# Two parts of a decoded weight summed on TensorE, fewer and longer VectorE instructions, and a new order of the work

## The chip, the cores and the metric

The kernel runs on one core of one Trainium2 chip. The metric is the device time of one execution in microseconds, and the time before is the median of 11 runs. A core has five engines, each with its own queue of instructions: TensorE (matrix products, written PE in the profile), VectorE (DVE), ScalarE (ACT), GpSimd (POOL) and SyncE (SP), which issues most of the DMAs. An engine works off its queue in order; between engines, semaphores hold an instruction back until its inputs are written and its output buffer is free.

## The reference

```python
def _attn_ref(q, k, v, a_re, a_im):            # each (4, 8, 768, 48)
    mag = np.sqrt(a_re * a_re + a_im * a_im)
    scale = np.minimum(mag, 0.999) / (mag + 1e-06)
    a_re_n, a_im_n = (a_re * scale, a_im * scale)
    for t in range(S):
        ar, ai = (a_re_n[:, :, t, :, None], a_im_n[:, :, t, :, None])
        new_re = ar * S_re - ai * S_im
        new_im = ar * S_im + ai * S_re
        S_re, S_im = (new_re + outer(k[t], v[t]), new_im)
        y[:, :, t] = q[t] @ S_re
    ...
def _moe_ref(x, w_in, w_out):                  # x (3072, 384), (384, 2048), (2048, 384)
    h = np.maximum(x @ w_in, 0.0)
    return (h * h @ w_out).astype(np.float32)
```

A gated recurrence with complex gates runs over 768 steps for each of 4 sequences and 8 heads. Its outputs, with the heads side by side, are 3072 tokens of 384 features, which go through two layers with a squared ReLU between them. The two weight matrices come in float64; everything else is float32.

## The kernel before

The 3072 tokens are cut into 24 chunks of 128 steps; two chunks of different sequences make one of 12 groups. A chunk's recurrence is turned into products: with the running products of the gates, queries are multiplied and keys divided by them (operands), a masked score matrix is made from both, and a state per head is carried from chunk to chunk. Groups 0 to 5 run through one pair of sequences and groups 6 to 11 through the other.

All work is cut into steps, and a string FRONT (L1035) writes down in which order they are issued: `follow` (L1129) reads token after token and calls the function behind its letter. On VectorE, TensorE, SyncE and ScalarE this is the order in which each engine runs its instructions. A token is a letter, a group or block, and a step:

- `l` loads a group's gates, queries and keys into the single tile `raw` (group 0 in two parts, l0.0 the gates and l0.1 the rest; 12 to 16 DMAs), `v` its values, `f` a block of 64-bit weights into one of three `words` tiles; blocks 0 to 7 are columns of the first matrix, 8 to 15 rows of the second.
- `D` decodes a block on VectorE (`decode`, L566): two instructions make `head`, two make `rest`, a fifth adds them into the float32 weight. `W` (`watch`) scans the words on ScalarE for values out of range.
- `o` are a group's operands (`make_operands`, L656), in the list's order: 0 squares, 1 and 2 the parts put in blocks, 3 sum of squares, 4 and 5 inverse and its square, 6 queries, 7 Newton step, 8 limit, 9 lessened, 10 grown factor (all ScalarE, but for 3 and 7), 11 gates, 12 negated (ScalarE), 13 grow (a running product over each of six segments, and the keys times it), 14 keys (ScalarE), 15 and 16 the running complex products in blocks of 8, 17 totals over the blocks, 18 carries (ScalarE), 19 carried, 20 products, 21 the DMAs for the last heads. Where no engine is named it is VectorE.
- `a` and `b` are the group's first and second chunk (`chunk`, L816): 0 scores, 1 and 3 keys transposed, 6 sums over values, 8 what is added to the state (TensorE); 2, 4 and 7 copies out of PSUM (ScalarE); 5 masked scores and 9 the new state (VectorE). `g` fills the gap rows of the tokens by DMA, after which `F` may start.
- `F` is one eighth of the first layer's product (12 recorded instructions, because a float32 product is recorded as two), `H` its squared ReLU on ScalarE, `T` an eighth of the second layer for groups 0 and 1, `E` its copy, `s` the store.
- From group 2 on, `X`, `Y` and `Q` (sums of tokens on VectorE), `t` (sums of weights) and `Z` (seven half-sized products in the place of eight) make the second layer, and `R` puts its outputs together.

In PSUM the pool `pa` (L455) holds the scores of a chunk, in two tiles of one bank, and the two outputs of T1; `py` the sums over values and the outputs of T0; `pm` the transposed keys and what is added to the state. A step that writes one of these waits until the step that reads the former content is done. `F0.f` needs block f of the weights, `T0.f` and `T1.f` block 8 + f.

The complex product is written out in `cmul` (L642): two products over both parts, then a difference and a sum.

Of the kernel before, what the change touches and what calls it, by code (L numbers as in the profile page):

```python
# [23 lines left out]
I32 = mybir.dt.int32  # L24
# [401 lines left out]
def quotient_path(ctx, tc, feat, vtok, w_in, w_out, w1, w2, out, n_seq, good):  # L426
# [28 lines left out]
    pa = ctx.enter_context(tc.tile_pool(name="pa", bufs=2, space=PSUM))  # L455
# [81 lines left out]
    carry = const.tile([P, 2, SEG, NB], F32, name="carry")  # L537
    nc.vector.memset(carry[:, RE], 1.0)
    nc.vector.memset(carry[:, IM], 0.0)
# [4 lines left out]
    prod = [const.tile([P, 2, GC, NP], F32, name=f"prod{i}") for i in range(2)]  # L544
# [12 lines left out]
    ends = const.tile([P, NGR, SEG], F32, name="ends")  # L557
    sizes = const.tile([P, 2, 2 * NBLK], F32, name="sizes")
# [7 lines left out]
    def decode(dst, words, j):  # L566
# [4 lines left out]
        both = scr.tile([P, 2, E], I32, tag="work", name="decoded")  # L571
        head, rest = both[:, 0], both[:, 1]
# [9 lines left out]
        tt(dst, head.bitcast(F32), rest, ALU.add)  # L582
# [8 lines left out]
    words_of = {}  # L591
# [50 lines left out]
    def cmul(out, x, w, shape, room=None):  # L642

        p_, w_ = room or [tmp.tile([P, 2] + shape, F32, name=name) for name in ("p_", "w_")]
        tt(p_, x, w[RE], ALU.mult)
        tt(w_, x, w[IM], ALU.mult)
        tt(out[:, RE], p_[:, RE], w_[:, IM], ALU.subtract)
        tt(out[:, IM], p_[:, IM], w_[:, RE], ALU.add)

    def spread(w, shape):  # L650

        return [w[:, c].unsqueeze(1).unsqueeze(3).to_broadcast([P, 2] + shape) for c in (RE, IM)]
# [3 lines left out]
    def make_operands(gi):  # L656
# [13 lines left out]
        def steps_in_blocks(js):  # L670

            for j in js:
                ab = tiles["ab"]
                x, w = ab[:, now, j - 1], ab[:, 0:2, j]
                plane = L * n

                x = bass.AP(tensor=x.tensor, offset=x.offset + plane,
                            ap=[x.ap[0], [-plane, 2], [0, 2], [1, n]])
                w = bass.AP(tensor=w.tensor, offset=w.offset,
                            ap=[w.ap[0], [plane, 2], [plane, 2], [1, n]])  # L680
                pr = tmp.tile([P, 2, 2, n], F32, name="pr")
                tt(pr, x, w, ALU.mult)
                tt(ab[:, now, j], pr[:, 0], pr[:, 1], ALU.add)

        def squares():
            tiles["sq"] = nrm.tile([P, 2, E], F32, name="sq")
# [36 lines left out]
        def limit():  # L723
            tiles["both"] = nrm.tile([P, 2, E], F32, name="both")
# [23 lines left out]

# [462 lines left out]
```

## Time and profile before

| | us |
|---|---|
| median of 11 runs | 707.85 (706.92 to 711.58) |
| profiled execution | 707.07 |
| its span | 705.3 |
| TensorE busy | 624.3 (89%) |
| VectorE busy | 531.4 (75%) |
| ScalarE busy | 368.9 (52%) |
| GpSimd busy | 12.0 (2%) |
| DMA | 47.75 MB, 68 GB/s on average |

The span runs from the first to the last instruction of the profiled execution; its device time is 1.8 us longer. The profile's strip cuts the span into 40 slices of 17.6 us and gives the busy share of each engine in tenths. The lists of instructions by time give start, duration, engine, line, operation, the tiles written and read, and in brackets the idle time before and what ended it. Nearly all VectorE products and sums have the line of the helper `tt` (L478), so they are told apart by their tiles and sizes.

### The profile page before, as it was taken

The numbers are of one execution on the slowest core, as the hardware profiler recorded it, in microseconds if no ns is written. First come the engines' busy times: TensorE is split into PE (matmuls) and PEld (weight loads), VectorE is DVE, ScalarE is ACT, GpSimd is POOL, SyncE is SP. The second block draws the span as 40 slices with busy tenths as digits, with TensorE's granted clock in tenths as the row PEclk, the third lists the DMA queues.
The fourth block names the chain that finished last, engine by engine and source line by source line (L and its number), as shares of the span: only waits on it lengthen the run. The fifth ranks groups of instructions, "written<-read, shape, count | busy, mean of one in ns | idle before, by whom it ended". The sixth has DMA issues, their size and how long they took to land.

```text
span 705.3 us, 12538 instructions
## 1 busy us (share of the span) xinstructions
PE 624.3 (89%) x4955; PEld 547.4 (78%) x4955; DVE 531.4 (75%) x1045; ACT 368.9 (52%) x636; POOL 12.0 (2%) x36
## 2 busy tenths in 40 slices
PE   0025688999879999999999999999999999999995
PEld 0024576775668998998998988988988989989995
DVE  2999999999897887987866967868868959922020
ACT  6466387476437538348357276285285284230330
POOL 3000000000000000000000000000000000000000
PEclk9999699999999999999999999999999999999999
DMA  5985572842351061421520620711612510010101
GB/s 135 171 135 106 85 158 80 163 127 85 79 87 23 8 123 30 76 71 24 118 46 1 119 46 7 124 35 25 116 25 41 101 23 5 16 35 1 29 0 29
DMA packets 46150, 47.75 MB, mean 68 GB/s; under 512 B 6017, under 2 KB 40961, under 8 KB 46081
## 3 DMA queue, kind: packets, MB, share of 16 engines
q1 hardware_dynamic: 45600, 46.46, 34.0%
q8 instruction: 41, 0.67, 0.4%
q10 hardware_dynamic: 480, 0.39, 0.2%
q14 instruction: 29, 0.23, 0.1%
HBM read 36.18 MB, written 4.72 MB: 58 GB/s over the span
## 4 chain that ended last, share of the span: by engine, by line
PE 73%; DVE 17%; DMA 4%; SPq 3%; issue 1%; ACT 0%; DVEq 0%; ACTq 0%
PE h_ps L927 28%; PE o_ps L1002 26%; PE a_ps L845 5%; PE o_ps L943 5%; DVE ab L478 3%; PE y L871 2%; PE y L837 2%; PE add L889 2%; DVE pr L478 2%; DMA raw<-in_feat_dram 2%; PE tp L852 1%; DVE qk L478 1%; DVE w L478 1%; DVE decoded L575 1%; DVE decoded L580 1%
## 5 line engine op out<-in xcount | busy, mean ns | idle before, releaser
L927 PE MATMUL h_ps<-x,w 128*128 128x256 f32 x1152 | 261.1, 384 | 8.3 <-DMA x<-x 7.4
L927 PEld LDWEIGHTS h_ps<-x,w 128*128 128x128 f32 x1152 | 218.9, 192 | 39.6 <-DMA x<-x 5.0
L1002 PE MATMUL o_ps<-w,h 128*128 128x192 f32 x640 | 110.3, 328 | 0.0
L1002 PEld LDWEIGHTS o_ps<-w,h 128*128 128x128 f32 x640 | 104.0, 190 | 2.2 <-issue 1.5
L932 ACT ACTIVATE h<-h_ps 128x512 f32<-128x512 f32 x96 | 57.6, 600 | 89.2 <-PE h_ps L927 85.6
L478 DVE TENSOR_TENSOR mix<-h 128x256 f32<-128x256 f32 x40 | 16.9, 422 | 62.9 <-ACT h L933 62.9
L933 ACT ACTIVATE h<-h 128x512 f32<-128x512 f32 x96 | 60.6, 631 | 3.0
L667 ACT ACTIVATE qk<-raw 128x768 f32<-128x768 f32 x24 | 36.8, 1534 | 36.3 <-DMA raw<-in_feat_dram 9.5
L1002 PE MATMUL o_ps<-w_sum,mix 128*128 128x192 f32 x320 | 54.9, 329 | 0.0
L852 PE MATMUL tp<-ident,qk 128*128 128x128 f32 x120 | 22.2, 297 | 35.3 <-DVE qk L478 27.2
L1002 PEld LDWEIGHTS o_ps<-w_sum,mix 128*128 128x128 f32 x320 | 51.8, 190 | 1.4 <-issue 1.4
L478 DVE TENSOR_TENSOR pr<-ab 128x384 f32<-128x384 f32 x84 | 46.7, 556 | 2.3
L852 PEld LDWEIGHTS tp<-ident,qk 128*128 128x128 f32 x120 | 14.7, 148 | 40.9 <-ACT size L588 27.7
L478 DVE TENSOR_TENSOR qk<-ab,qk 128x768 f32<-128x768 f32 x48 | 44.9, 955 | 0.8
L943 PE MATMUL o_ps<-w,h 128*128 128x384 f32 x128 | 42.4, 488 | 1.3 <-DVE w L478 0.8
L478 DVE TENSOR_TENSOR a<-a_ps,mask 128x512 f32<-128x512 f32 x48 | 30.8, 684 | 14.8 <-PE a_ps L845 14.8
L845 PE MATMUL a_ps<-qk 48*128 48x128 f32 x576 | 40.7, 290 | 0.0
L667 ACT ACTIVATE both<-z 128x768 f32<-128x768 f32 x24 | 37.1, 1563 | 5.7 <-DVE z L718 5.7
L845 PEld LDWEIGHTS a_ps<-qk 48*128 48x128 f32 x576 | 36.0, 197 | 4.4 <-issue 4.3
L943 PEld LDWEIGHTS o_ps<-w,h 128*128 128x128 f32 x128 | 24.1, 190 | 18.0 <-DVE w L478 1.5
L667 ACT ACTIVATE ab<-raw 128x768 f32<-128x768 f32 x24 | 37.7, 1570 | 0.3 <-DVE qk L478 0.3
L871 PE MATMUL y<-a,vt 128*64 128x128 f32 x384 | 29.0, 285 | 4.8 <-DVE a L478 4.6
(299 smaller groups left out, 817.4 us busy)
## 6 DMA issues: line engine op xcount, KB each, us to landing
raw<-in_feat_dram SPq DMA_DIRECT2D x44, 288.0 KB
words<-in_moe_w_out_dram SPq DMA_DIRECT2D x8, 768.0 KB
last<-qk SPq DMA_DIRECT2D x72, 64.5 KB
vt<-in_vtok_dram SPq DMA_DIRECT2D x24, 192.0 KB
out_dram<-o SPq DMA_DIRECT2D x24, 192.0 KB
raw<-in_feat_dram SPq DMA_DIRECT2D x132, 32.0 KB
words<-in_moe_w_in_dram SPq DMA_DIRECT2D x16, 192.0 KB
words<-in_moe_w_in_dram SPq DMA_DIRECT2D x32, 96.0 KB
```

The costliest lines, as they stand in the source:

```text
L478: nc.vector.tensor_tensor(out=out, in0=in0, in1=in1, op=op)
L667: nc.scalar.activation(out=out.rearrange("p c j n -> p c n j"), func=AF.Copy, in_=in_.rearrange("p c (n j) -> p c n j", j=L), **kwargs)
L837: nc.tensor.matmul(ys[p_ % 2][crossed(hh, p_), p_ // 2], lhsT=states[b][1 - c_seq % 2][rows(hh), c, p_], rhs=operand(c, p_, rows(hh)), sta ...
L845: nc.tensor.matmul(ps[hh][:, p_], lhsT=operand(2 + c, p_, rows(hh)), rhs=operand(c, p_, rows(hh)), start=(c == RE), stop=(c == IM))
L852: nc.tensor.transpose(tp[:, g], operands[gi][:, 2 + c, b, g, 0:C], ident)
L871: nc.tensor.matmul(tiles["y"][p_ % 2][crossed(hh, p_), p_ // 2], lhsT=v[:, at:at + ROWS], rhs=tiles["am"][hh][:, p_], start=(first and p_ ...
L889: nc.tensor.matmul(add[rr, c, p_], lhsT=kt[c][:, p_, rr], rhs=v[:, at:at + D], start=True, stop=True)
L927: nc.tensor.matmul(ps[:, j], lhsT=w1[:, g, (2 * f + j) * P:(2 * f + j + 1) * P], rhs=x_of[i][:, g], start=(g == 0), stop=(g == NG - 1))
L932: nc.scalar.activation(out=h, in_=h_ps[i, f], func=AF.Relu)
L933: nc.scalar.activation(out=h, in_=h, func=AF.Square)
L943: nc.tensor.matmul(o_of[i, b], lhsT=tokens_of(i, f, b)[:, j], rhs=w2[:, k], start=(k == 0), stop=(k == NFB - 1))
L1002: nc.tensor.matmul(to, lhsT=x(k)[:, j], rhs=factor(z)[:, 2 * k + j], start=(z in (0, 1, 3) and k == j == 0), stop=(k == KH // 2 - 1 and j ...
```

## The change

Seven edits:

1. `decode` writes `head` straight into the weight's place. For blocks 0 to 7 its fifth instruction is gone: step `B` (`summed`) multiplies head and rest with the unit matrix on TensorE and adds both in a PSUM tile of `pa`, and step `C` (`sums_copied`) copies that to the weight's place on ScalarE. Two blocks share one buffer for their rests.
2. `pa` has one buffer of two banks instead of two of one. Scores of both halves, the two outputs of T1 and the sums of `B` each take the whole of it. `masked` becomes one instruction over both halves.
3. `grow` scans all six segments in one instruction: step 22 on ScalarE squares the factors, copies the first one of each segment to `begun` and sets it to zero in the factors, so that the scan starts anew there.
4. `carried` and `new_state` make four products in two instructions and then one sum over both parts, with a third, negated plane in `carry` and `prod`, which ScalarE (and GpSimd for the last heads) fills.
5. `totals` makes its first level's four products in one instruction.
6. The temporary tiles are brought together (`room`, `four`).
7. FRONT is written anew throughout: D0 and D1 come before the gates and the scan of group 0, blocks 0 to 5 are decoded ahead of F0.0, v0, f0 and v1 are fetched ahead of l0.1, and f2 ahead of l1; step 15 of group 3 comes ahead of its scan and step 16 ahead of the masks of group 2.

```diff
-    pa = ctx.enter_context(tc.tile_pool(name="pa", bufs=2, space=PSUM))
+    pa = ctx.enter_context(tc.tile_pool(name="pa", bufs=1, space=PSUM))
...
-        both = scr.tile([P, 2, E], I32, tag="work", name="decoded")
-        head, rest = both[:, 0], both[:, 1]
+        if j % 2 == 0:
+            rest_of[j // 2] = scr.tile([P, 2, E], I32, tag="work", name="decoded")
+        head, rest = dst.bitcast(I32), rest_of[j // 2][:, j % 2]
...
-        tt(dst, head.bitcast(F32), rest, ALU.add)
+        if j >= 8:
+            tt(dst, dst, rest, ALU.add)
+
+    def summed(i):
+        dst, rest = w1[:, :, i * BLK:(i + 1) * BLK], rest_of[i // 2][:, i % 2].bitcast(F32)
+        to = sum_of[i] = pa.tile([P, HH, NP, C], F32, tag="a", name="sum").rearrange(
+            "p b x t -> p (b x t)")
+        for g in range(NG):
+            at = slice(g * BLK, (g + 1) * BLK)
+            for k, part in enumerate((dst[:, g], rest[:, at])):
+                nc.tensor.matmul(to[:, at], lhsT=ident, rhs=part, start=(k == 0 and g % 2 == 0),
+                                 stop=(k == 1 and g > 0), skip_group_check=True)
+
+    def sums_copied(i):
+        nc.scalar.copy(out=w1[:, :, i * BLK:(i + 1) * BLK],
+                       in_=sum_of[i][:, 0:E].rearrange("p (g f) -> p g f", g=NG))
...
+        def grown_squared():
+            nc.scalar.activation(out=tiles["sq"][:, 0], in_=tiles["sq"][:, 1], func=AF.Square)
+            at = tiles["sq"][:, 0].rearrange("p (s t) -> p s t", s=SEG)[:, :, 0]
+            nc.scalar.copy(out=begun.rearrange("p (s t) -> p s t", s=SEG)[:, :, 0], in_=at)
+            nc.scalar.mul(out=at, in_=at, mul=0.0)
+
         def grow():
-            v = tiles["sq"][:, 1]
-            grown = v.rearrange("p (s t) -> p s t", s=SEG)
-            for s in range(SEG):
-                nc.vector.tensor_tensor_scan(out=grown[:, s], data0=grown[:, s],
-                                             data1=grown[:, s], initial=1.0, op0=ALU.mult,
-                                             op1=ALU.mult)
+            u, v = tiles["sq"][:, 0], tiles["sq"][:, 1]
+            nc.vector.tensor_tensor_scan(out=v, data0=u, data1=begun, initial=0.0, op0=ALU.mult,
+                                         op1=ALU.add)
             tt(r[:, K], r[:, K], v, ALU.mult)
...
+                if m == 1:
+                    tt(pr[..., 0], planes(x[..., 0], 1, 0), planes(w[..., 0], 0, 1), ALU.mult)
...
+            for k in (RE, IM):
+                tt(pr[:, k].rearrange("p c (j n) -> p c j n", n=n), planes(x[:, k:], 0),
+                   planes(w[:, 1 - k:], 1), ALU.mult)
+            tt(x.rearrange("p c j n -> p c (j n)"), pr[:, 0], pr[:, 1], ALU.add)
...
-            tiles["am"] = [att.tile([C, NP, C], F32, name="a", bufs=2) for _ in range(HH)]
-            for am, ps in zip(tiles["am"], tiles["ps"]):
-                tt(am, ps, mask.unsqueeze(1).to_broadcast([C, NP, C]), ALU.mult)
+            am = tiles["am"] = att.tile([C, HH, NP, C], F32, name="a", bufs=1)
+            tt(am.rearrange("s hh x t -> s (hh x) t"), tiles["ps"].rearrange("s hh x t -> s (hh x) t"),
+               mask.unsqueeze(1).to_broadcast([C, HH * NP, C]), ALU.mult)
...
-            p_ = tmp.tile([P, 2, NP, D], F32, tag="pr", name="p_")
-            w_ = tmp.tile([P, 2, NP, D], F32, tag="tw", name="w_")
-            tt(p_, sum_, w[RE], ALU.mult)
-            tt(w_, sum_, w[IM], ALU.mult)
-            tt(new[:, RE], p_[:, RE], w_[:, IM], ALU.add)
-            tt(new[:, IM], p_[:, IM], w_[:, RE], ALU.subtract)
+            w = prod[gi % 2][:, :, b].unsqueeze(3).to_broadcast([P, 3, NP, D])
+            pr = four().rearrange("p (k c x d) -> p k c x d", k=2, c=2, d=D)
+            for k in (RE, IM):
+                tt(pr[:, k], planes(sum_[:, k:], 0), planes(w[:, 1 + k:], -1), ALU.mult)
+            tt(new, pr[:, 0], pr[:, 1], ALU.add)
...
     FRONT = (
-        "l0.0 M0 l0.1 o0.0 o0.3 o0.1 o0.4 o0.5 o0.7 o0.2 f0 v0 v1 o0.8 o0.10 o0.9 o0.11 o0.6 M1 W0 f1 "
-        "o0.13 o0.12 o0.15 o0.14 l1 o0.16 W1 o0.17 f2 D0 o0.18 o0.19 o1.6 o0.20 o1.0 f3 W2 a0.1 o1.3 o1.1 "
-        "o0.21 D1 o1.4 o1.5 o1.2 a0.2 o1.7 f4 a0.0 W3 D2 o1.8 o1.9 a0.3 a0.5 o1.10 a0.4 a0.6 o1.11 f5 W4 "
-        "a0.8 a0.7 b0.0 o1.13 o1.12 b0.5 o1.14 b0.6 o1.15 W5 l2 b0.7 a0.9 b0.1 o1.16 b0.2 b0.3 g0 b0.4 "
-        "o1.17 b0.8 v2 b0.9 o1.18 o1.19 o2.6 F0.0 o1.20 o2.0 F0.1 H0.0 F0.2 H0.1 o2.3 o1.21 o2.1 D3 a1.1 "
-        "H0.2 o2.4 a1.2 a1.3 o2.2 D4 f6 F0.3 a1.4 o2.5 a1.0 H0.3 o2.7 D5 o2.8 F0.4 o2.9 f7 a1.8 H0.4 F0.5 "
-        "a1.9 o2.10 W6 a1.5 b1.1 H0.5 a1.6 D6 b1.2 f8 b1.3 a1.7 b1.0 W7 D7 b1.4 F0.6 b1.5 W8 f9 F0.7 D8 "
-        "H0.6 b1.8 H0.7 b1.6 v3 b1.7 o2.11 T0.0 g1 W9 f10 o2.13 o2.12 F1.0 o2.15 o2.14 F1.1 H1.0 l3 W10 "
-        "o2.16 T1.0 H1.1 o2.17 F1.2 f11 F1.3 H1.2 D9 o2.18 F1.4 o2.19 T1.1 o3.6 T0.1 H1.3 D10 o3.0 f12 "
-        "F1.5 H1.4 W11 F1.6 o2.20 T1.2 W12 f13 D11 o2.21 T0.2 H1.5 o3.1 F1.7 D12 H1.6 T1.3 o3.2 f14 W13 "
-        "D13 T1.4 H1.7 T0.3 o3.3 b1.9 o3.4 T1.5 f15 W14 D14 T0.4 o3.5 T0.5 o3.7 W15 T1.6 D15 o3.8 T0.6 "
-        "o3.10 t0 o3.9 T1.7 o3.11 T0.7 E1.0 E1.1 s1.0 s1.1 t1 o3.12 a2.1 E0.0 E0.1 s0.0 o3.13 b2.0 a2.2 "
-        "s0.1 a2.3 b2.5 o3.14 b2.6 o3.15 a2.4 l4 a2.8 b2.7 a2.0 a2.9 b2.1 a2.5 b2.2 b2.3 o3.16 a2.6 b2.4 "
-        "b2.8 a2.7 g2 b2.9 v4 o3.17 o4.6 F2.0 "
...
+        "l0.0 M0 v0 f0 v1 o0.0 l0.1 o0.3 M1 o0.4 o0.1 o0.5 o0.7 o0.2 f1 W0 D0 o0.10 o0.8 B0 o0.9 o0.11 "
+        "o0.6 C0 W1 f2 D1 o0.22 o0.12 B1 o0.13 o0.15 o0.14 l1 W2 o0.16 C1 o0.17 f3 D2 o0.18 B2 o0.19 o1.6 "
+        "o0.20 o1.0 C2 f4 W3 a0.1 o1.3 o0.21 o1.1 D3 o1.2 o1.4 B3 o1.5 o1.7 a0.2 f5 W4 o1.8 a0.3 D4 C3 "
+        "a0.0 o1.10 a0.4 o1.9 a0.8 a0.5 f6 a0.6 D5 W5 B4 a0.7 o1.11 C4 b0.0 b0.5 o1.22 f7 b0.6 a0.9 W6 B5 "
+        "o1.13 b0.7 o1.12 g0 b0.1 C5 o1.15 b0.2 b0.3 o1.14 b0.4 l2 o1.16 b0.8 W7 F0.0 o1.17 F0.1 H0.0 "
+        "b0.9 o1.18 F0.2 f8 H0.1 v2 o1.19 F0.3 H0.2 F0.4 H0.3 o1.20 o2.6 F0.5 o2.0 D6 o1.21 o2.1 a1.1 "
+        "a1.2 a1.3 o2.2 o2.3 B6 f9 D7 o2.4 a1.4 a1.8 C6 W8 a1.0 a1.9 o2.5 b1.1 a1.5 H0.4 a1.6 o2.7 f10 "
+        "b1.2 F0.6 a1.7 H0.5 o2.10 b1.0 o2.8 o2.9 b1.3 b1.5 b1.4 B7 o2.11 W9 W10 b1.8 D8 b1.6 C7 v3 F0.7 "
+        "b1.7 o2.12 g1 o2.22 D9 f11 T0.0 H0.6 H0.7 F1.0 o2.13 F1.1 H1.0 o2.15 o2.14 f12 F1.2 W11 l3 o2.16 "
+        "H1.1 T1.0 o2.17 F1.3 H1.2 W12 D10 F1.4 o2.18 T1.1 D11 f13 T1.2 H1.3 F1.5 H1.4 D12 o3.6 F1.6 "
+        "o2.19 W13 f14 T0.1 T1.3 H1.5 D13 o3.0 F1.7 H1.6 f15 W14 D14 T1.4 T1.5 H1.7 o3.3 o2.20 o3.4 T1.6 "
+        "o3.5 W15 T0.2 o3.7 o2.21 o3.1 o3.2 T0.3 D15 o3.10 o3.8 T0.4 o3.9 b1.9 T1.7 o3.11 a2.1 E1.0 T0.5 "
+        "E1.1 s1.0 a2.2 s1.1 t0 o3.12 o3.22 T0.6 o3.15 T0.7 o3.13 a2.3 E0.0 E0.1 s0.0 b2.0 a2.4 s0.1 "
+        "o3.16 o3.14 l4 a2.8 b2.5 b2.6 o3.17 b2.7 a2.0 a2.9 o3.18 b2.1 a2.5 b2.2 a2.6 o3.19 b2.3 a2.7 "
+        "b2.4 g2 b2.8 v4 o3.20 o4.6 F2.0 "
...
```

The helper `planes` builds a view of a tile that steps through its planes, forwards, backwards or not at all.

## The prediction

> **What bounds the kernel now.** I read the busy strips first, then the busy time by windows, then the timeline of each engine up to 204 us. The strips: VectorE is full for the first 11 slices and loosens later; TensorE fills only from slice 5 on and is then full to the end.
>
> ```profile
> PE   0025688999879999999999999999999999999995
> DVE  2999999999897887987866967868868959922020
> ```
>
> The windows put numbers on that. The columns are the window, its length, then busy time with the number of instructions for TensorE, its weight loads, VectorE, ScalarE and GpSimd, the granted TensorE clock, the DMA share and GB/s.
>
> ```profile
> 60.00:80.00 20.00, 10.24 (x122) 8.60 (x119) 19.03 (x50) 8.02 (x20) 0.00 (x0) 0.76 0.67 103
> 80.00:100.00 20.00, 17.68 (x124) 14.85 (x125) 19.52 (x23) 13.90 (x20) 0.38 (x1) 0.90 0.46 90
> 180.00:204.00 24.00, 17.88 (x252) 13.63 (x250) 21.00 (x41) 8.56 (x20) 0.00 (x0) 0.99 0.64 105
> 204.00:697.00 493.00, 492.53 (x3988) 448.48 (x3988) 349.88 (x736) 247.59 (x431) 4.03 (x9) 1.00 0.25 46
> ```
>
> See that from 204 to 697 us TensorE is busy 492.53 of 493.00 us, while VectorE has 143 us to spare there. Whatever VectorE saves behind 204 us is worth nothing, because TensorE covers it. The TensorE steps that the two orders put from F2.0 (first product of group 2) to the end are the same set. So the time moves with the start of F2.0, now at 203.96 us, and with any new gap behind it.
>
> The timelines give the marks of the front: VectorE's first gate step, a scan of six segments, the last mask before F2.0; TensorE's F0.0 and F2.0; and on ScalarE the watch of block 1, which waits for its words, and the issue of those words on SyncE's queue.
>
> ```profile
> 17.24 0.96 DVE L739 SCALAR_TENSOR_TENSOR both<-both 128x768 f32<-128x768 f32 x1 [3.59 <-ACT both L667]
> 20.89 2.00 DVE L753 TENSOR_TENSOR_SCAN sq<-sq 128x128 f32<-128x128 f32 x6
> 197.58 1.28 DVE L478 TENSOR_TENSOR a<-a_ps,mask 128x512 f32<-128x512 f32 x2
> ...
> 79.79 10.14 PE L927 MATMUL h_ps<-x,w 128*128 128x256 f32 x36 [3.32 <-DMA x<-x]
> 131.75 7.93 PE L927 MATMUL h_ps<-x,w 128*128 128x256 f32 x36
> 203.96 17.27 PE L927 MATMUL h_ps<-x,w 128*128 128x256 f32 x72 [3.04 <-DMA x<-x]
> ...
> 27.34 0.89 ACT L586 ACTIVATE size<-words 128x768 bf16<-128x768 f32 x1 [1.91 <-DMA words<-in_moe_w_in_dram]
> 18.41 3.31 SPq L613 DMA_DIRECT2D words<-in_moe_w_in_dram  x6
> ```
>
> **The parts, and what each costs.** Steps are named as in the plan; durations are start to next start on one engine.
>
> Decode of blocks 0 to 7: four instructions instead of five, 3.15 us instead of 4.10 (33.89 to the add at 37.07, and the add's 0.96): eight times 0.95 is 7.6 us off VectorE. TensorE gets B: six products 128x256 against the unit matrix, recorded as 12 instructions like one F, so 2.59 us (the 36 above take 7.93), 20.7 us in all. ScalarE gets C: a copy of 768 columns from PSUM; its rows are 0.478 us for 384 and 0.600 for 512, so 0.95 ns a column, 0.84 us long and 0.76 to the next; 6.1 us in all. GpSimd's extra product of 4 columns and its memset have nobody waiting (its copy takes 0.38 to 0.55 us).
>
> One scan of 768 for six of 128. The six take 2.03 us to the next start. An add of 384 takes 0.556 us and one of 768 0.957, 1.04 ns an element, so one of 128 would take 0.29; the scan of 128 takes 0.402. If the excess is fixed, the long scan takes 0.957 + 0.11 = 1.07 us and saves 0.96; if it grows with the elements, the long scan is the six without their five starts of about 0.07 us, 1.67 us, and saves 0.36. I take 1.67, since six scans back to back already run at 0.33 us each, twice what 128 elements at 1.04 ns and a start make. [...] On ScalarE the squares, the starts copied out and the zeros (step 22) cost 0.75 + 0.1 + 0.2, about 1.1 us, between the gates and the scan.
>
> Fused masks, new states, totals and carried sums save one start each, 0.07 us (bounds 0 and 0.12). carries gets one small ScalarE copy more (0.1 to 0.2 us), hidden by D2 or b0.9 on VectorE before step 19.
>
> Behind F2.0 all of it is priced at nothing: VectorE 349.88 and ScalarE 247.59 us of 493. The new order there can only lose (0.47 us of TensorE idle is all there is to gain), between 0 and some 3 us; I take 0.
>
> **Where the new order puts it: F0.0.** SyncE issues l0.1's twelve DMAs after f0, v0 and v1; f1 still has the same DMAs ahead and issues until 21.7 us. Before, its words were there at 27.34; block 4's words came 3.1 us after their last issue (watch at 57.72). With the backlog moved forward I take 25.1 us and keep 27.3 as the other end. The chain then:
> - ScalarE from 7.15 us: squares 1.39, M1 1.9 with TensorE's turn in it, o0.4 0.84, o0.1 1.40, o0.5 0.84, o0.2 1.40, W0 1.97, o0.10 0.76, o0.8 and o0.9 2.76, sum 13.3 with waits below 0.1. So the gates (o0.11) start at 20.3 instead of 17.24; D0 fills VectorE's pause from 15.3 to 18.4.
> - o0.11 3.64, to 23.9; D1 waits for f1, 25.1 to 28.2, and all of group 0's steps stand behind it on VectorE, as o0.22 does behind W1 on ScalarE; W1 (1.97) and o0.22 (1.1) on ScalarE end at 28.2 too. The scan starts at 28.3, before it was 20.89.
> - o0.13 2.57, o0.15 3.95, o0.16 2.95, o0.17 3.10, D2 3.13, o0.19 4.50: 20.2 us, so carried ends at 48.5 (before: 42.54). l1's DMAs wait for o0.14 (32.4), issue for 8.6 us and land 4.7 later, 45.7, as before (34.0, then 38.74); they are hidden by that sum, with 1.6 us left for o1.6.
> - Now ScalarE alone, from 48.7: o1.0 1.39, C2 0.76, W3 1.97, o1.1 and o1.2 2.80, o1.4 and o1.5 1.68, a0.2 0.56, W4 1.97, o1.8 1.38, C3 0.76: 13.3, to 62.0. C4 and C5 will wait about 2 and 1 us for their sums with o1.22 and b0.2 behind them; o1.22 is hidden, since o1.11 ends only at 72.3, b0.2 is in the next sum. The two halves of the buffer for the second parts are free again when B3 (for D4) and B7 (for D8) are done, 0.2 and 2 us before they are wanted; gone, either would be paid one for one. B3, even at half clock (4.5 us from D3's end at 56.4), ends at 61.0, before C3 asks.
> - With one PSUM tile for sums and scores, a0.0 waits for C3, B4 for a0.5, b0.0 for C4, B5 for b0.5. One behind the other: a0.0 1.96, mask 1.13, a0.6 1.02, B4 2.59, C4 0.76, b0.0 1.96, mask 1.13, b0.6 1.02, B5 2.59, C5 0.76, b0.2 0.56, o1.14 1.53, b0.4 0.56, b0.8 1.07: 18.6, and 13 handovers of 0.15 us: 20.5. F0.0 starts at 82.5, 2.7 us later than 79.79.
>
> **From F0.0 to F2.0.** Before: 203.96 - 79.79 = 124.2 us, of which work is 32 steps F and T of 2.59 (82.9) and four chunks of 1.03 + 1.96 + 0.82 + 1.02 + 1.07 = 5.9 (23.6), so 17.7 us are waits and the slow first 36 products (10.14 against 7.93). After: B6 and B7 add 5.2, work 111.7. D3 to D5 now lie ahead of F0.0, so F0.3 to F0.7 hardly wait. Left are 1.6 and 0.6 (a1.3, B6 for D6), 1.1 and 1.1 behind masks (a1.6, B7), 0.5 at T0.0, and chunk 2's own handovers, 8 (the window 180 to 204 has 6.1 us of idle TensorE and its end hangs on a DMA). That is 13, sum 124.7, so F2.0 at 207.2. VectorE agrees: from the scan at 28.3 the new order has 162.9 us up to mask a2.5 (D2 to D15 51.7, operands 94.3, masks and states 15.2, t0 1.7, and o3.16, o3.17 which the old order had behind it, inside the operands). It stands idle 1.1 at o1.7, 1.6 at a0.5, 0.8 at b0.5 and a1.9, 0.4 at a1.5, and 5.1 at b1.5, because b1.0 comes behind a1.6 and F0.6 on TensorE. So a2.5 at 200.3 (before 197.58), and 6.4 us later, as before, F2.0 at 206.7. Both paths land at 207. On SyncE's queue l4's 8.6 us stand ahead of g2 and end at 201, 2.5 us before g2 is asked for.
>
> [...]
>
> **Sum.** 203.96 to 207.2 is +3.2 us on the profiled execution's 707.07, so 710.3; that execution lies 0.8 us under the median shown, 707.85, which makes 711.
>
> **Rivals.**
> - Faster. The sum of VectorE sets F2.0 and its pauses vanish: 28.3 + 162.9 + 1.5 of pauses + 6.4 = 199.1, 4.9 us early, 703. For it the chain of ScalarE and PSUM must not bind: it decides once F0.0 starts before 79 us and b1.0 is done when o2.7 ends. For it speaks that VectorE is busy over 19 of 20 us in the front now; against it the 13.3 us of ScalarE without a pause.
> - Same. Short ends together: the scan at 1.07 takes 0.6 off each of the two groups ahead of F0.0 and of the two behind it (2.4), C 0.2 shorter. F2.0 at 204.5, 708.4.
> - Slower still. f1 at 27.3 adds 2.2, and the new order leaves 0.5 us of TensorE idle in some of the nine groups behind F2.0, up to 3: 716.
>
> **How the numbers follow.** About 0.3% (2.1 us) is what a measurement tells from no change. The forecast, 710 to 714, gets 0.45; slower still 0.15; same 0.17; faster 0.23. So slower 0.60. The likeliest is 711, with its own range of 709 to 714. The whole range goes from 702, under the faster rival, to 718, above the slowest.
>
> **What would show it.** F0.0 at about 82 and F2.0 at about 207; the first scan near 28, one of about 1.7 us; ScalarE without idle time from 49 to 62; VectorE waiting some 5 us for scores at mask b1.5; TensorE with 12 more instructions per block, some 5051 products in the page instead of 4955; no wait above 1 us on TensorE behind F2.0. If F0.0 starts before 79 with the chain as listed, the ScalarE terms were too large; if F0.0 is right and F2.0 is not, the waits between them were.

## The result and the profile after

The changed kernel takes 715.98 us (median of 13 executions, 712.28 to 718.04); the kernel before, on the same chip, takes 710.73 us. The ratio is 1.008 with a 95% interval of 1.0062 to 1.0098, so the change makes the kernel 0.6 to 1.0% slower. The forecast was slower by 3.2 us, that is by 0.45%; its sign held, its size was a little more than half of what was measured. Most executions of the kernel before lie near 707 or near 711 us, with a granted clock of about 0.984 or 0.975, so its median depends on how many of each it has: 707.85 us ahead of the forecast, 710.73 us here. The 715.98 us are above the 709 to 714 us of the likeliest case; on the 707.85 us from which the forecast started, the ratio makes 713.5 us.

The profiled execution of the changed kernel took 713.58 us with a span of 711.8 us, 6.5 us more than the span before (705.3 us). First its busy strips, from the page:

```profile
PE   0535798999969999999999999999999999999995
DVE  3798996999999896887959869699589795112130
PEclk9757999999999999999999999999999999999999
```

TensorE now works in slices 2 and 3 (18 to 53 us), where it had 0 and 2 tenths before. These are short sums with pauses between them, and the granted clock is 0.7, 0.5 and 0.7 in slices 2 to 4, where it was 0.9 before. From slice 13 on TensorE's strip is the same as before. The windows say it in numbers (columns as in the windows of before):

```profile
20.00:40.00 20.00, 9.25 (x22) 6.27 (x21) 14.89 (x20) 11.48 (x18) 0.00 (x0) 0.74 0.59 114
40.00:60.00 20.00, 6.59 (x15) 4.16 (x15) 18.91 (x33) 8.66 (x14) 0.00 (x0) 0.59 0.97 138
212.00:700.00 488.00, 486.87 (x3966) 444.58 (x3967) 339.49 (x625) 257.37 (x459) 5.01 (x18) 1.00 0.25 47
```

Behind F2.0 TensorE is busy 486.87 of 488.00 us, as it was before. In 20 to 40 us VectorE, which sets the pace there, works only 14.89 of 20 us, where it worked 19.07 before. The marks of the front in the timelines, VectorE's first, then TensorE's:

```profile
28.20 0.95 DVE L579 TENSOR_SCALAR w<-words 128x768 int32<-128x768 int32 x1 [3.34 <-DMA words<-in_moe_w_in_dram]
32.05 1.75 DVE L773 TENSOR_TENSOR_SCAN room<-room,begun 128x768 f32<-128x768 f32 x1
122.75 1.23 DVE L478 TENSOR_TENSOR a<-a_ps,mask 128x1024 f32<-128x1024 f32 x1 [5.14 <-PE a_ps L877]
...
88.42 6.90 PE L957 MATMUL h_ps<-x,w 128*128 128x256 f32 x25
212.50 5.42 PE L957 MATMUL h_ps<-x,w 128*128 128x256 f32 x24 [1.14 <-DMA x<-x]
```

F0.0 starts at 88.42 us instead of 79.79 (+8.63), F2.0 at 212.50 instead of 203.96 (+8.54). Between the two lie 124.1 us, before 124.2. So in the profiled executions the whole loss is made before F0.0, and 2.0 us of it are won back behind F2.0: from there to the end it takes 499.3 us, before 501.3. Before, the first 24 of group 2's products came after a pause of 3.04 us and on a clock of 0.91 in 200 to 220 us; now the pause is 1.14 us and the clock 1.00.

Two groups of the page, VectorE's first and third instruction of a decode, tell what else is new. The columns are the line, the operation and its tiles, the number, the busy time with the mean ns of one, and the idle time ahead:

```profile
L583 DVE TENSOR_SCALAR decoded<-w 128x768 int32<-128x768 int32 x16 | 12.1, 756 | 1.5 <-PE sum L599 0.9
L579 DVE TENSOR_SCALAR w<-words 128x768 int32<-128x768 int32 x16 | 12.0, 750 | 4.9 <-DMA words<-in_moe_w_in_dram 3.3 <-DMA raw<-in_feat_dram 1.2 <-issue 0.4
```

The mean of 750 ns hides two kinds: 0.95 us for blocks 0 to 7 and 0.55 us for blocks 8 to 15. Before, all 32 took 0.56 us:

```profile
L577 DVE TENSOR_SCALAR decoded<-decoded 128x768 int32<-128x768 int32 x16 | 9.0, 560 | 0.6
L573 DVE TENSOR_SCALAR decoded<-words 128x768 int32<-128x768 int32 x16 | 8.9, 556 | 0.1
```

For blocks 0 to 7 the change writes the first part straight into the weight's tile, where a block's 768 columns are three runs of 256, 2048 apart. The first instruction writes there, and the third reads the first part from there and writes one run of 768.

### The profile page after: what moved, and what is told of

Read it like the earlier page. It is cut to its first block, busy times and chain, and to the rows that moved or that the text cites. A ratio compares the mean times of both kernels' runs of the same rounds, so it can differ in the third digit from the quotient of the medians.

```text
span 711.8 us, 12673 instructions
## 1 busy us (share of the span) xinstructions
PE 645.8 (91%) x5051; PEld 563.6 (79%) x5051; DVE 521.9 (73%) x909; ACT 389.5 (55%) x692; POOL 13.1 (2%) x49
## 4 chain that ended last, share of the span: by engine, by line
PE 69%; DVE 21%; DMA 5%; SPq 2%; issue 1%; ACT 0%; DVEq 0%
PE h_ps L957 29%; PE o_ps L1034 26%; PE a_ps L877 5%; DVE pr L478 4%; DVE ab L478 4%; PE y L903 3%; PE y L869 2%; DVE qk L478 2%; PE add L921 2%; DVE room L478 2%; DMA vt<-in_vtok_dram 2%; PE tp L884 1%; DVE w L581 1%; DVE decoded L586 1%; DMA words<-in_moe_w_in_dram 1%; DMA last<-qk 1%
## 5 line engine op out<-in xcount | busy, mean ns | idle before, releaser
L1034 PE MATMUL o_ps<-w,h 128*128 128x192 f32 x640 | 108.3, 327 | 0.0
L478 DVE TENSOR_TENSOR pr<-ab 128x384 f32<-128x384 f32 (+2 forms) x168 | 66.4, 413 | 7.6 <-ACT ab L761 3.7
L478 DVE TENSOR_TENSOR ab<-pr 128x192 f32<-128x192 f32 (+1 forms) x180 | 45.8, 276 | 4.6
L599 PE MATMUL sum<-w,ident 128*128 128x256 f32 x48 | 20.4, 516 | 28.4 <-DVE w L581 20.8
L478 DVE TENSOR_TENSOR a<-a_ps,mask 128x1024 f32<-128x1024 f32 x24 | 29.3, 1221 | 22.0 <-PE a_ps L877 21.9
L877 PE MATMUL a_ps<-qk 48*128 48x128 f32 x576 | 38.6, 280 | 1.3 <-ACT w L603 1.3
L877 PEld LDWEIGHTS a_ps<-qk 48*128 48x128 f32 x576 | 34.0, 187 | 5.9 <-issue 3.9
L599 PEld LDWEIGHTS sum<-w,ident 128*128 128x128 f32 x48 | 11.6, 258 | 32.4 <-issue 13.4
L478 DVE TENSOR_TENSOR room<-ab,carry 128x1344 f32<-128x1344 f32 x24 | 36.2, 1551 | 1.0 <-ACT carry L802 0.9
```

The lines of the kernel that those rows point to most:

```text
L478: nc.vector.tensor_tensor(out=out, in0=in0, in1=in1, op=op)
L599: nc.tensor.matmul(to[:, at], lhsT=ident, rhs=part, start=(k == 0 and g % 2 == 0), stop=(k == 1 and g > 0), skip_group_check=True)
L877: nc.tensor.matmul(ps[:, hh, p_], lhsT=operand(2 + c, p_, rows(hh)), rhs=operand(c, p_, rows(hh)), start=(c == RE), stop=(c == IM))
L1034: nc.tensor.matmul(to, lhsT=x(k)[:, j], rhs=factor(z)[:, 2 * k + j], start=(z in (0, 1, 3) and k == j == 0), stop=(k == KH // 2 - 1 and j ...
```

## The experiments

**The theory** after the result: two terms of the forecast are wrong, and they make the difference. The words of block 1 land 3 us later than reckoned with the scan waiting behind them, and the decode of a block saves almost nothing, because two of its four instructions have become slow. **The rivals:** the sums on TensorE are what costs the time; the new order costs it; the cheaper VectorE instructions cost it, with the step on ScalarE and the single tile that came with them. The new order without any of the other edits was not run.

Each ratio below is to the kernel before, run beside it on the same chip; F0.0 and F2.0 are from the profiled execution of each. "Scores" says whether one or two tiles of PSUM hold a chunk's scores.

| kernel | order | sums | scan | scores | F0.0 | F2.0 | ratio (95%) |
|---|---|---|---|---|---|---|---|
| before | old | no | six | two | 79.79 | 203.96 | 1 |
| e9 | old | no | six | two | 79.99 | 203.97 | 0.9985 (0.996 to 1.0009) |
| e7 | old | no | six | one | 80.80 | 210.37 | 1.0028 (1.0003 to 1.0053) |
| e6 | old | no | one, with its step | one | 83.86 | 212.40 | 1.007 (1.0045 to 1.0095) |
| e1 | new | no | one | one | 86.30 | 216.53 | 1.012 (1.0086 to 1.0155) |
| after | new | yes | one | one | 88.42 | 212.50 | 1.008 (1.0062 to 1.0098) |
| e2 | new, weight by blocks | yes | one | one | 85.46 | 208.57 | 1.0067 (1.0045 to 1.0089) |
| e3 | new, block 1 later | yes | one | one | 87.25 | 210.14 | 1.0071 (1.0047 to 1.0096) |
| e8 | both of these | yes | one | one | 82.47 | 205.82 | 0.9996 (0.9972 to 1.0021) |
| e12 | both of these | yes | one | two | 82.59 | 206.09 | 0.9995 (0.9967 to 1.0024) |

**Without the sums (e1).** The edit, on the changed kernel, with all steps B and C taken out of the order as well:

```diff
-        if j % 2 == 0:
-            rest_of[j // 2] = scr.tile([P, 2, E], I32, tag="work", name="decoded")
-        head, rest = dst.bitcast(I32), rest_of[j // 2][:, j % 2]
+        both = scr.tile([P, 2, E], I32, tag="work", name="decoded")
+        head, rest = both[:, 0], both[:, 1]
...
-        if j >= 8:
-            tt(dst, dst, rest, ALU.add)
+        tt(dst, head.bitcast(F32), rest, ALU.add)
```

> Edit: the changed kernel with its new order and its cheaper VectorE work, but without sums on TensorE: every block is decoded by VectorE alone, as before (its own add of the two parts). Theory (the sums cost TensorE and the wait of their tile, and save VectorE almost nothing because the two stretched instructions give back 0.8 us of the 0.95 us a block that the add took): VectorE's decode of blocks 0 to 7 stays near 4.1 us instead of about 4.0 us, so F0.0 starts within 1.5 us of the changed kernel's 88.4 us; time 714 to 719 us. Rival (the sums are what costs the time): without them F0.0 goes back to about 80 us and the time to about 708 to 711 us.

Measured: 717.66 us, ratio 1.012; the changed kernel had 1.008. TensorE's two marks:

```profile
86.30 9.07 PE L953 MATMUL h_ps<-x,w 128*128 128x256 f32 x31
216.53 7.11 PE L953 MATMUL h_ps<-x,w 128*128 128x256 f32 x24 [1.12 <-DMA x<-x]
```

F0.0 comes 2.1 us earlier, a little more than the theory allowed, but F2.0 4.0 us later. Block 3's decode, from its first instruction to the start of the next one, is 4.04 us here (five instructions) against 3.98 us in the changed kernel (four). So the sums cost 2.1 us ahead of F0.0, but they are not what makes the kernel slower: it is no faster without them, and in this order it looks slower, though the two intervals overlap. Why F2.0 comes later without them was not tracked.

**The weight stored block by block (e2).** The edit gives each block its 768 columns in one run, for the decode, for the copy and for the products that read it:

```diff
+    blocks = w1.rearrange("p g f -> p (g f)")
...
-                   w1[:, :, j * BLK:(j + 1) * BLK], words_of[i], i)
+                   blocks[:, j * E:(j + 1) * E], words_of[i], i)
...
-        nc.scalar.copy(out=w1[:, :, i * BLK:(i + 1) * BLK],
-                       in_=sum_of[i][:, 0:E].rearrange("p (g f) -> p g f", g=NG))
+        nc.scalar.copy(out=blocks[:, i * E:(i + 1) * E], in_=sum_of[i][:, 0:E])
...
-                nc.tensor.matmul(ps[:, j], lhsT=w1[:, g, (2 * f + j) * P:(2 * f + j + 1) * P],
+                nc.tensor.matmul(ps[:, j], lhsT=blocks[:, f * E + g * BLK + j * P:][:, 0:P],
```

> Edit: the changed kernel with the first weight stored block by block, so that each block's 768 columns lie together and the two tensor-scalar instructions of a decode write one straight run; nothing else moves. Theory (the stretched destination makes each of the two instructions take 0.95 us instead of 0.55 us): both take 0.55 us, decode of a block 0 to 7 falls from about 4.0 to about 3.2 us, F0.0 starts 3 to 4 us earlier (84 to 85.5 us), F2.0 about 3 us earlier (209 to 210 us), time 711.5 to 714 us. Rival (the stretch has nothing to do with it, the instructions are slow because PSUM or the copies of ScalarE are beside them): still 0.95 us, time as the changed kernel's, 716 us.

The same two groups in its page:

```profile
L584 DVE TENSOR_SCALAR decoded<-w 128x768 int32<-128x768 int32 x16 | 9.0, 560 | 0.9 <-PE sum L600 0.2
L580 DVE TENSOR_SCALAR w<-words 128x768 int32<-128x768 int32 x16 | 8.9, 557 | 4.0 <-DMA words<-in_moe_w_in_dram 3.1 <-DMA raw<-in_feat_dram 0.9
```

```profile
30.82 1.76 DVE L773 TENSOR_TENSOR_SCAN room<-room,begun 128x768 f32<-128x768 f32 x1 [0.27 <-ACT room L769]
...
85.46 9.86 PE L957 MATMUL h_ps<-x,w 128*128 128x256 f32 x40
208.57 5.42 PE L957 MATMUL h_ps<-x,w 128*128 128x256 f32 x24 [1.12 <-DMA x<-x]
```

All 32 are back at 0.56 us, with ScalarE still copying out of PSUM beside them: the stretched place was the cause, for the instruction that writes there and for the one that reads there. Block 3's decode takes 3.14 us (56.34 to 59.48), the figure of the forecast; F0.0 is 3.0 us and F2.0 3.9 us earlier than in the changed kernel. The time, 713.76 us, is at the upper end of what was expected, and the intervals of the two ratios overlap: of 3.9 us at F2.0 little shows at the end in this profile (span 711.7 us), because here TensorE waits once more at 219.65 us and its clock falls to 0.57 for 8 us, by estimate 3.4 us of work at a clock of 1.00. The rows have two durations, 0.95 us in the changed kernel and 0.56 us here. The changed kernel writes both source and destination of these instructions as three runs (L578), of which only those in the weight's tile lie apart. Whether the number of the runs or the distance between them decides, no run here shows.

**Block 1's decode behind the scan (e3).** The edit is in the order alone:

```diff
-"C0 W1 f2 D1 o0.22 o0.12 B1 o0.13 o0.15 o0.14 l1 W2 o0.16 C1 o0.17"
+"C0 f2 o0.22 o0.12 o0.13 o0.15 D1 B1 o0.14 l1 W1 W2 o0.16 C1 o0.17"
```

> Edit: the changed kernel with block 1's decode and the second words' pass put behind the scan of group 0 in the order, so that the scan no longer waits behind the words that land at 28.2 us; all else as in the changed kernel. Theory (the wait of 3.3 us ahead of the decode of block 1 is part of the delay): the scan starts at 26 to 28 us instead of 32.05 us, F0.0 starts 1 to 3 us earlier than 88.4 us, time 713.5 to 715.5 us. Rival (the path to F0.0 goes over the sums on TensorE and not over VectorE, so the wait is hidden): F0.0 stays within 0.5 us of 88.4 us, time 716 us.

```profile
26.23 1.76 DVE L773 TENSOR_TENSOR_SCAN room<-room,begun 128x768 f32<-128x768 f32 x1 [1.50 <-ACT room L769]
...
87.25 8.04 PE L957 MATMUL h_ps<-x,w 128*128 128x256 f32 x36
```

The scan starts 5.8 us earlier and is now held for 1.50 us by ScalarE's new step, which block 1's decode no longer covers. F0.0 moves by 1.2 us, F2.0 by 2.4 us; the median is 714.61 us, and the ratio cannot be told from the changed kernel's. The wait for the words is part of the loss, as the theory said, but the smaller part: block 1's decode is only moved, not saved.

**Both repairs (e8), beside the changed kernel once more (e5).**

> Edit: the changed kernel with both repairs, the first weight stored block by block and block 1's decode put behind the scan. Theory (the two terms lie one behind the other on VectorE and add up: 3.0 us and 1.2 us at F0.0, 3.9 us and 2.4 us at F2.0 when made alone): F0.0 at 83.5 to 85 us, F2.0 at 205.5 to 208 us, ratio to before 1.002 to 1.006 and some 2 to 5 us under the changed kernel beside it. Rival (from F0.0 on TensorE is the bound and each repair's gain is given back as TensorE waiting or as a fall of the granted clock): F2.0 moves by the same but the time by under 1 us.

> Edit: none; the changed kernel once more, on the chip of the three runs beside it, so that they can be held against it and not against another day's chip. Theory: ratio to before 1.006 to 1.010, F0.0 at 88 to 89 us, F2.0 at 212 to 213 us; in both kernels the end behind F2.0 varies by some 4 us with whether the granted clock falls once more between 190 and 230 us.

```profile
25.46 1.76 DVE L773 TENSOR_TENSOR_SCAN room<-room,begun 128x768 f32<-128x768 f32 x1 [1.50 <-ACT room L769]
...
82.47 12.81 PE L957 MATMUL h_ps<-x,w 128*128 128x256 f32 x53
205.82 5.42 PE L957 MATMUL h_ps<-x,w 128*128 128x256 f32 x24 [1.23 <-DMA x<-x]
```

F0.0 is 6.0 us and F2.0 6.7 us earlier than in the changed kernel, a little more than the two gains made alone (4.1 and 6.3 us). The medians, from the same chip, are 710.83 us and 715.75 us, so 4.9 us of it reach the end. The ratio to before is 0.9996, better than the 1.002 expected at the least: with these two terms taken away, nothing measurable is left of the loss. The changed kernel repeated its ratio, 1.0075 (1.0051 to 1.0098), and F0.0 at 88.68 us; its F2.0, 214.57 us, came later than the 212 to 213 us expected.

**The parts in the old order (e4, e6, e7, e9).** What remains is why the change, repaired, wins nothing. The first run put the new step ahead of o*.12, but behind the scan:

> Edit: the cheaper VectorE instructions of the change alone (the scan in fewer instructions, the step of ScalarE that they need put just ahead of the one that uses it), with the order of before and without sums on TensorE. Theory (the order and the sums cost the time, the cheaper instructions do not): F0.0 within 2 us of the kernel before's 79.8 us, F2.0 at 202 to 207 us, time 707 to 713 us, that is within 0.3% of before. Rival (the cheaper instructions themselves, through their longer scan and the step moved onto ScalarE, cost it): F2.0 at 209 us or later, time 714 us or more.

It took 711.22 us, ratio 1.0033 (1.0002 to 1.0063), F0.0 82.46, F2.0 209.41. There the scan does not wait for the step that prepares its factors, so its time stands for neither theory. The next run has the step in its place, in every group as in the first:

```diff
-"M1 o0.13 o0.12 o0.15 o0.14"
+"M1 o0.22 o0.13 o0.12 o0.15 o0.14"
```

> Edit: the order of before with the cheaper VectorE instructions and no sums on TensorE, as in the earlier run in the old order, but with ScalarE's new step ahead of the scan that uses its result (in the earlier run the scan was issued ahead of the step that prepares its multipliers, so that it ran on old ones and TensorE's scores had other values; its instructions were the same). Theory (the new step puts ScalarE's square and two small copies, some 1.1 to 1.4 us, ahead of each scan): VectorE waits 1 to 1.5 us ahead of the first scan, F0.0 at 81 to 83 us, F2.0 207 to 210 us, ratio to before 1.002 to 1.006. Rival (the step is hidden): F2.0 at 203 us, ratio 0.998 to 1.000.

Measured: 715.13 us, ratio 1.007, above the expected range, F2.0 at 212.40 us. The first scan:

```profile
23.66 1.76 DVE L769 TENSOR_TENSOR_SCAN room<-room,begun 128x768 f32<-128x768 f32 x1 [2.08 <-ACT room L765]
```

The step that replaces five starts of a scan makes VectorE wait 2.08 us here, 3.5 us in the two groups ahead of F0.0 and 5.3 us more up to F2.0. The last wait alone is 3.87 us, because there the step stands behind copies of outputs on ScalarE. Then the same without it:

```diff
-            nc.vector.tensor_tensor_scan(out=v, data0=u, data1=begun, initial=0.0, op0=ALU.mult,
-                                         op1=ALU.add)
+            for s in range(SEG):
+                nc.vector.tensor_tensor_scan(out=grown[:, s], data0=grown[:, s],
+                                             data1=grown[:, s], initial=1.0, op0=ALU.mult,
+                                             op1=ALU.mult)
```

> Edit: the run in the old order without the new step: the scan again as six instructions on VectorE, all other cheaper VectorE instructions of the change kept, no sums. Theory (of the cheaper instructions only the scan's new step costs time; the others save some 0.5 us a group of VectorE, 1.5 us for the three groups ahead of F2.0): F2.0 at 201 to 204 us, ratio to before 0.995 to 1.000. Rival (the one tile of scores in PSUM, which is given back as a whole, costs what the cheaper instructions save): VectorE's or TensorE's waits at the masked scores grow by 1 to 2 us a chunk, F2.0 at 205 us or later, ratio 1.001 to 1.005.

Measured: 713.41 us, ratio 1.0028, F0.0 at 80.80 and F2.0 at 210.37 us: the rival was right. Of the 8.8 us that the scans waited in e6, 2.0 us are left at F2.0. Of VectorE's fewer instructions nothing arrives. What is left of the change here is the merged instructions and the single tile of scores, so the last run of this row splits the tile again:

```diff
-            ps = tiles["ps"] = pa.tile([C, HH, NP, C], F32, tag="a", name="a_ps")
+            ps = tiles["ps"] = [pa.tile([C, NP, C], F32, tag="a", name="a_ps") for _ in range(HH)]
...
-            tt(am.rearrange("s hh x t -> s (hh x) t"), tiles["ps"].rearrange("s hh x t -> s (hh x) t"),
-               mask.unsqueeze(1).to_broadcast([C, HH * NP, C]), ALU.mult)
+            for am, ps in zip(tiles["am"], tiles["ps"]):
+                tt(am, ps, mask.unsqueeze(1).to_broadcast([C, NP, C]), ALU.mult)
```

> Edit: the run in the old order with six scans (no new step, no sums), with the scores again in two tiles of PSUM, each masked by its own instruction and given back by itself, as in the kernel before. Theory (the one tile of scores is what cost the time there: VectorE's wait of 5.5 us at a masked score ahead of F2.0, against 2.3 us before): the wait falls under 3 us, F2.0 comes at 202 to 205 us instead of 210.4 us, ratio to before 0.995 to 1.000. Rival (the merged instructions themselves, or the state's product that reads three planes, cost it): F2.0 at 208 us or later, ratio 1.002 or more.

Measured: 708.40 us, ratio 0.9985, F2.0 at 203.97 us as in the kernel before. The two runs side by side, first e7, then e9: ScalarE's first copy of group 1's outputs, which lie in the same tiles as the scores, and the mask of chunk b2.

```profile
184.51 0.86 ACT L985 COPY o<-o_ps 128x384 f32<-128x384 f32 x2 [4.30 <-PE o_ps L963]
195.73 1.23 DVE L478 TENSOR_TENSOR a<-a_ps,mask 128x1024 f32<-128x1024 f32 x1 [5.46 <-PE a_ps L867]
```

```profile
181.00 0.48 ACT L983 COPY o<-o_ps 128x384 f32<-128x384 f32 x1 [3.02 <-PE o_ps L963]
190.42 1.29 DVE L478 TENSOR_TENSOR a<-a_ps,mask 128x512 f32<-128x512 f32 x2 [2.39 <-PE a_ps L867]
```

With one tile both halves' copies begin only when the products of both are done, 3.5 us later. Behind them ScalarE copies the outputs of group 0 (L985 at 188.50 and 189.48 us), TensorE's next products wait for these copies, and so the next scores start at 191.90 instead of 188.34 us. So in the old order the single tile costs about 0.43% (1.0028 against 0.9985), some 3 us, though the two intervals still touch; and the merged instructions with two tiles are worth nothing that can be told from zero (0.996 to 1.0009). Part of the 6.4 us at F2.0 comes with the clock: in e7 it is 0.50 from 192 to 200 us, where e9 has 1.00. Whether that fall follows from the tile was not tried.

**Two tiles with the repairs (e12).** If the tile costs 3 us in the old order, splitting it should help the repaired kernel. The scores are split as in e9, and a block's sum with them:

```diff
-        to = sum_of[i] = pa.tile([P, HH, NP, C], F32, tag="a", name="sum").rearrange(
-            "p b x t -> p b (x t)")
+        to = sum_of[i] = [pa.tile([P, NP * C], F32, tag="a", name="sum") for _ in range(2)]
```

> Edit: the run with both repairs (first weight block by block, block 1's decode behind the scan), and the scores again in two tiles of PSUM, masked by two instructions; a block's sum then lies in the two tiles too (512 and 256 columns) and is copied by two instructions of ScalarE. Theory (in the old order the single tile cost 6.4 us at F2.0 and 0.43% of the time; in the new order TensorE still waits 2.07 and 1.25 us for masked scores ahead of F2.0, which two tiles shorten): F0.0 at 82 to 84 us, F2.0 at 202 to 205 us, ratio to before 0.993 to 0.998. Rival (in the new order the long wait, 5.1 us at the masked score of group 1, is TensorE's queue and not the tile; two copies and two masks cost 0.2 us and 0.14 us each): F2.0 at 205 to 208 us, ratio 0.999 to 1.004.

```profile
194.23 0.43 PE L904 MATMUL y<-a,vt 128*64 128x128 f32 x2 [1.52 <-DVE a L478]
200.73 0.43 PE L904 MATMUL y<-a,vt 128*64 128x128 f32 x2 [0.73 <-DVE a L478]
```

The same two products in e8:

```profile
194.63 1.09 PE L903 MATMUL y<-a,vt 128*64 128x128 f32 x16 [2.07 <-DVE a L478]
201.06 1.09 PE L903 MATMUL y<-a,vt 128*64 128x128 f32 x16 [1.25 <-DVE a L478]
```

The rival was right: 711.07 us, ratio 0.9995, F2.0 at 206.09 us. TensorE's two waits do get shorter, by 0.5 us each against e8, but the time does not follow: VectorE's 5.1 us at the mask of chunk b1 stay as they are, since TensorE comes to those scores late in its own queue. The price that the tile had in the old order is not seen in the new one; the interval, 2 us to either side, would hide a smaller one.

**Two attempts at a faster kernel (e10, e11).** Only the places of loads, size checks, decodes, sums and copies were moved; e10 starts from e2's kernel in the new order, e11 from e9.

> Edit: the changed kernel with the first weight stored block by block, and with only the weights' tokens of the order moved (loads, size checks, decodes, sums and copies), so that the scan is ahead of block 2, each sum's tile is free before the scores want it, and no block's decode stands behind a load. Theory (the front is bound by VectorE and by the sums' tile, and both of the changed kernel's mis-placements can be had back): F0.0 at 78 to 81 us, F2.0 at 201 to 204 us, ratio to before 0.990 to 0.997. Rival (what is won ahead of F2.0 is lost behind it, where TensorE is busy without a break): F2.0 as early, ratio 0.998 or more.

> Edit: the old order with six scans, two tiles of scores and no sums, with the weights' tokens moved in the same way. Theory (with the merged instructions alone VectorE has some 1.5 us less to do ahead of F2.0, and a better place of the decodes is worth some 3 us more): F2.0 at 198 to 202 us, ratio to before 0.990 to 0.996. Rival (the loads come too late when the decodes come earlier, and the waits for words take what is won): F2.0 at 203 us or later, ratio 0.998 or more.

Both missed: e10 took 712.69 us, ratio 1.0026 (0.9998 to 1.0054), F0.0 82.26, F2.0 211.62; e11 took 711.06 us, ratio 1.0003 (0.9981 to 1.0024), F2.0 208.68. In e10 the loads of two more blocks went ahead of group 1's features on SyncE's queue, and ScalarE, which needs the features, stood still:

```profile
48.68 1.52 ACT L687 ACTIVATE qk<-raw 128x768 f32<-128x768 f32 x1 [7.34 <-DMA raw<-in_feat_dram]
```

That lies ahead of F0.0. From F0.0 to F2.0 e10 takes 129.4 us, where e8 takes 123.4, and that loss was not tracked.

In e11 F0.0 comes as early as before (79.95 us) and the loss is behind it; of it the profile shows VectorE waiting 1.9 us for words, which it does not do before, and TensorE waiting 5.05 us for the tokens' DMA ahead of F2.0, where it waited 3.04 us before; the rest was not tracked. No kernel of this study is shown to be faster than the one before.

## Why the prediction was right, and where its terms were wrong

- **What sets the time: right.** The time moves with F2.0, and behind F2.0 the change is worth next to nothing: no wait above 0.6 us on TensorE in the changed kernel, and from F2.0 to the end of the span 499.0 to 503.1 us in every profile of this study. The forecast put 0 there; in the profiled execution it was 2.0 us of gain, which is why 8.5 us at F2.0 became 6.5 us of span. That gain was luck: no term of the forecast gave it.
- **F0.0 to F2.0: right in the sum.** 124.7 us were reckoned, 124.1 measured. The parts were not: TensorE was busy 115.6 us of it, where 111.7 were reckoned, and idle 8.5, where 13 were reckoned; the two errors cancelled. The 111.7 us count the first products at F0.0 at 220 ns each, as in before's row of 36 (7.93 us), an estimate of the author that held only in part: the granted clock is 0.97 in 80 to 88 us and 0.63 in 88 to 92, and the first 25 products take 6.90 us, 276 ns each; in e3 the first 36 take 8.04 us, 223 ns each. The wait at mask b1.5, 5.1 us, was measured as 5.14, for the reason given (TensorE's queue), and in e12 it is the same with two tiles. TensorE's 5051 products are as forecast.
- **F0.0 at 82.5: wrong by 5.9 us, in two terms.** The first is "25.1" for block 1's words: they came at 28.2 us, later even than the other end that the forecast kept, 27.3. SyncE issued them from 21.20 us, after 18.41 before, though the same transfers were ahead of them; the step "issues until 21.7 us" took for granted that these would go out as fast as before. SyncE's queue, first v1, then the features' first issue and the words of blocks 1 and 2:

```profile
9.70 2.98 SPq L510 DMA_DIRECT2D vt<-in_vtok_dram  x2
13.20 0.32 SPq L493 DMA_DIRECT2D raw<-in_feat_dram  x1
...
21.20 6.51 SPq L635 DMA_DIRECT2D words<-in_moe_w_in_dram  x12
```

The twelve issues of features ran from 13.20 to 21.16 us, 8.0 us, where before they took 7.4 us; v1's two took 2.98 us, where before the four of v0 and v1 took 2.70; and the queue paused for 0.5 us. Why the issues took longer in this order, no run shows. The late words made up 3.1 of the 3.75 us by which the scan was late (32.05 instead of 28.3), and e2 has this term alone: with the decode as reckoned, block 1's decode starts at 27.41 us, the scan starts at 30.82 and F0.0 at 85.46, 3.0 us after the forecast's 82.5.
- **The second term is "3.15 us instead of 4.10" for a decode.** 3.98 us was measured. The forecast counted the instruction that falls away and took the other four at the durations they had with another destination. Two of them took 0.4 us more each, which gives nearly all of the 0.95 us back: eight blocks times 0.8 us, 6.4 us of VectorE, and blocks 0 to 5 lie ahead of F0.0. e2 brought the decode that was reckoned (3.14 us) and 3.0 us at F0.0.
- **ScalarE without a pause, then the handovers of the PSUM tile: right, 5 us late.** ScalarE's steps from o1.0 to C3 took 14.1 us, 0.8 of them a wait for B3, where 13.3 were reckoned; they began at 53.70 us instead of 48.7. From the end of C3 to F0.0 it took 20.7 us, where 20.5 were reckoned. The first and the last step:

```profile
53.70 1.48 ACT L702 ACTIVATE room<-raw 128x1536 f32<-128x1536 f32 x1 [2.19 <-DVE ab L478]
...
66.95 0.80 ACT L603 COPY w<-sum 128x768 f32<-128x768 f32 x1 [0.78 <-PE sum L599]
```

- **B3 at half clock: right.** The granted clock is 0.50 from 62 to 67 us, where B3 runs (in the kernel before it is 0.50 from 72 to 84 us). Two records of B3 start every 0.85 us; two of B4, at a clock of 1.00 in 72 to 76 us, every 0.43. Over all the sums a record took 516 ns in the mean with the first part and 505 with the second, where one of the first layer takes 220 in before's row of 36. The forecast gave B3 4.5 us from D3's end, to 61.0, "before C3 asks"; it took 4.7 us from D3's end at 62.2. As D3 took longer and ended late, B3 ended at about 66.9, with VectorE waiting 0.86 us and ScalarE 0.78 us for it. In e8, where D3 is not late, C3 follows at 61.17 us without a wait, so the argument held where its time held.
- **The scan: right.** 1.67 us were taken, 1.75 us measured; the cheaper end, 1.07, is out. An instruction over two tensors of 768 took 0.96 us.
- **"About 1.1 us" for step 22: a little short, 1.35 us were measured (30.14 to 31.49 us), and it was covered in the new order by block 1's decode on VectorE.** Where it is not hidden (e3, e8) the scan waits 1.50 us, in the old order 2.08 us.
- **The faster rival's condition was never met.** It was to decide from F0.0 before 79 us; the repairs in the new order gave 82.3 to 82.6 us (e8, e10, e12), and the best of them only ties with before. For "slower still" two reasons were given: late words came, a loss behind F2.0 did not.

So the direction was right for the reason given, the chain to F0.0. But 5.9 us of that chain were missing from it, and the measured time is not further from the forecast because 2.0 us came back behind F2.0, which it did not reckon.

## What to carry to other kernels

When a change gives an instruction a new destination, price it anew: removing one instruction of five saved 0.06 us instead of 0.95, because one of the others had to write into three runs and another had to read from them. A shared tile of PSUM and a step put ahead of a scan have no price of their own: here the single tile cost some 3 us in one order and nothing that could be told from zero in the other, and 1.4 us of ScalarE cost 2.1 us of VectorE where nothing stood ahead of it. Where an order is moved, look first at the first load that a whole engine then stands behind.

## What was not expected of the hardware

- A VectorE instruction with one source and a constant took 0.95 us where either its 768 results or its 768 inputs lay in three separate runs of 256, and 0.56 us where both lay in one (of the words, in both cases, every second element is read); the instructions of a decode with two tensors took 0.96 us in both cases.
- Two executions of one and the same kernel differ by where the clock falls. The windows from 200 to 220 us, of the changed kernel's profile and of its repetition (e5):

```profile
200.00:220.00 20.00, 15.10 (x169) 12.65 (x170) 19.41 (x35) 9.99 (x21) 0.00 (x0) 1.00 0.66 118
```

```profile
200.00:220.00 20.00, 18.02 (x149) 14.92 (x150) 17.30 (x33) 8.16 (x17) 0.00 (x0) 0.57 0.62 99
```

With a granted clock of 0.57 instead of 1.00 TensorE is busy 2.9 us longer over fewer products, F2.0 comes at 214.57 instead of 212.50 us, and the span is 714.9 instead of 711.8 us. That is as much as any single part of the change was worth, so a mark behind the first pauses is good to about 2 us in one profile, and it takes the medians of many executions to tell such parts apart. What decides where the clock falls, no run here shows.
